# A fixed turn on TensorE for convolution backward and weight-gradient jobs, with reloads moved ahead of transposes and swapped spectra read from memory

## The chip, the cores and the metric

The kernel runs on one core of a Trainium2 chip. The metric is the device time of one execution in microseconds (us); the median of several runs is given, and one further view, the profile, is of a single execution. The engines are named as in the profile: PE (TensorE, matrix multiply), PEld (its weight loads), DVE (VectorE), ACT (ScalarE), POOL (GpSimd) and SP (SyncE, which here only issues DMAs).

## The reference

The program computes the forward pass of four residual layers, and all gradients: for the input, for the two convolution inputs and kernels, and for the two matrices of the dense layer. Sequence length S is 2048, width D is 448, hidden width F is 1792, all in bf16.

```python
def _A_ref(q, k, v, shift_k, ssm_k, ssm_D):
    k_shift = sum of 4 shifted copies of k, each times a column of shift_k
    kv = k_shift * v
    # causal convolution over 2048 steps, by FFT of length 4096
    y = irfft(rfft(kv, 4096) * rfft(ssm_k, 4096))[:2048] + kv * ssm_D
    return q * y
def _B_ref(x, w1, w2):
    return silu(x @ w1) @ w2

x = A_q
x = x + _A_ref(layernorm(x), A_k, A_v, A_shift_k, A_ssm_k, A_ssm_D)
x = x + _B_ref(layernorm(x), B_w1, B_w2)
x = x + _A_ref(layernorm(x), ...same...)
x = x + _B_ref(layernorm(x), B_w1, B_w2)
outputs: x, and the gradients of A_q, A_k, A_v, A_shift_k, A_ssm_k, A_ssm_D, B_w1, B_w2
```

The convolution branch doesn't depend on x, so its result y (in the code `Y`) is computed once and used by both A layers; the gradients of both A layers meet in one array, `gYb`, before a single backward convolution.

## The kernel before, in words

The program has three parts that follow one another in the code.

**Prefix** (`_ssm_prefix`): the forward convolution. A two-stage transform turns the convolution kernel and kv into spectra `spec_K` and `spec_KV`, which are kept in device memory, and `Y` stays in SBUF.

**Main** (`Main.run`): the sequence is cut into 4 chunks of 512 steps (c = 0 to 3), each of 4 tiles of 128 (tl = 0 to 3). A first loop over c does the first A and B layers; it stores the pre-activation of the dense layer as `DT_d` and the activations `aT`, turned by a transposing DMA, as `A_d`. A second loop over c does the second A and B layers forward (`h`, `out`) and at once backward (`ga`, `gn`, with L = 1). A third loop over c does the backward of the first A and B layers (`ga`, `gn`, with L = 0); I call it the **second backward**. In one chunk of it:

- `load_d` reloads a half of `DT_d` into a `dTl` buffer (3 buffers, tag "D"), and `slope` turns it into the derivative of silu: 4 ACT instructions in place. The code calls the first half of chunk c+1 `e0`, the second half `d1`.
- `ga` runs 7 steps fp: PE multiplies (`ps_g`), ACT copies the product out of PSUM (`ghp`, one buffer), DVE multiplies by the derivative (`ghT`). After steps 3 and 6 `store_turned` issues two transposing DMAs on SP's queue and, delayed, the store to `GH_d`.
- `gn` multiplies by the other matrix (`ps_n`), and for each of the 4 tiles runs the backward of both layernorms: ACT `lb_u` and `lb_v`, DVE the rest. The last DVE write of interest is `gYb`.

**Suffix** (`_ssm_suffix`): the backward convolution from `gYb` and the **weight-gradient jobs**. The convolution goes through these steps: stage 1 (`ps_s` with `M1s`, 16 steps n2, one for each 128 rows, n2 = 12 to 15 being chunk 3); 7 groups of transposes (`ps_tr`); then 7 passes cp, each a `spectrum` (`ps_s` with `Gsb`) and an `inverse`, which multiplies the spectrum by the stored ones (DVE `pa`, `pb`) and transforms back (`ps_v`); then `gK`, `gkv`, the shift-kernel gradient `sk`, and a DVE loop for the gradient of k. A job is one row block of a weight gradient: a 512 KB `dstat` tile is loaded from `A_d` or `GH_d` on SP's queue, and 16 matmuls (`ps_d`, 128x448) follow. There are 28 jobs for B_w2 (`_gw2`: moving operands `X` and `GO`) and 28 for B_w1 (`_gw1`: `mov3` and `mov1`), 896 matmuls in all. In the text of the kernel the jobs stand after the convolution.

The order of instructions on each engine is made when the program is built: a scheduler takes instructions by priority as their inputs become free in its own model, and each engine then runs its list strictly in that order. `tc.issue_after(ins)` puts the instructions of a block behind `ins` on that engine's list, without a wait. Before the change no such order links convolution and jobs; the scheduler put job matmuls where it saw room: 55 of the 896 stand ahead of stage 1 of the convolution. DMAs of SP and of ACT go through hardware queues; those of POOL through a software queue.

Of the kernel before, what the change touches and what calls it, by code (L numbers as in the profile page):

```python
# [13 lines left out]
ALU = mybir.AluOpType  # L14
# [19 lines left out]
def make_fft_consts():  # L34
# [44 lines left out]
    GiBc = np.roll(GiBc, 64, axis=0)  # L79
# [127 lines left out]

def _fft_stage1(k, n2, rhs, A1, psum):
    nc = k.nc
    ps = psum.tile([P, 2, 512], FP32, name="ps_s1", **k.pt["s1"])  # L210
    for c in range(2):
        nc.tensor.matmul(ps[:, c, :D], lhsT=k.M1sb[:, n2, c, :], rhs=rhs, start=True, stop=True)
    _copy(nc, k.bal.pick(2 * D), A1[:, :, :, n2, :].rearrange("p dh c ds -> p c dh ds"), ps[:, :, :D].rearrange("p c (dh ds) -> p c dh ds", ds=4))

# [249 lines left out]
class Main:  # L464
# [98 lines left out]
    def h(self, c, L, nT, half, hold):  # L563
# [3 lines left out]
        hold.append((aT, dT))  # L567
        for ft0, n, at in ((0, 2, 1), (2, 2, 0), (4, 2, None), (6, 1, None)) if half == 0 else ((7, 1, None), (8, 2, 1), (10, 2, 0), (12, 2, None)):
# [20 lines left out]
        if L == 1:  # L589
            self.store_turned(k.A_d[1], aT, c, half)  # L590

# [24 lines left out]
    def ga(self, c, L, gT, dT, mid=None):  # L616
        nc, k = self.nc, self.k
        ghT = [self.td.tile([P, NF // 2, 512], BF16, name=f"ghT{h}", tag="T", bufs=3) for h in range(2)]
        for fp in range(NF // 2):
            ps = k.psum.tile([P, 2, 512], FP32, name="ps_g", tag="mm", bufs=2)  # L620
            self.contract(ps, self.w2T, gT, 2 * fp, 2, None if fp == 6 else (fp + 1) % 2)
            if fp == 2 and mid:
                mid()
# [3 lines left out]
            k.bal.add("dve", -0.5)  # L627
            for u in ((0, 1),) if fp != 3 else ((0,), (1,)):
# [3 lines left out]
            if fp in (3, 6):  # L632
                hh = (fp - 3) // 3
                self.store_turned(k.GH_d[L], ghT[hh], c, hh)
        return ghT
# [71 lines left out]
    def run(self):  # L707
# [21 lines left out]
        for c in range(4):  # L729
            gb, gT = self.g_pre(c, 1)  # L730
            self.h(c, 1, nT, 1, cur)
# [3 lines left out]
            self.turn_plain(c)  # L735
            if c == 3:
                d0 = self.load_d(0, 0)
                self.slope(d0)
                k.GO = k.wk.tile([P, NT, D], BF16, name="GO", tag="WA")
                with self.tc.issue_after(k.d_load.ins):  # L740
                    nc.sync.dma_start(out=k.GO[:], in_=_pm(k.grad_out[0]))
            box = []
            ghT = self.ga(c, 1, gT, cur, (lambda: box.append(self.b_pre(c + 1, 3))) if c < 3 else None)
# [5 lines left out]
            else:  # L749
                d1, e0 = self.load_d(0, 1), self.load_d(1, 0)  # L750
# [5 lines left out]
        for c in range(4):  # L756
# [3 lines left out]
            ghT = self.ga(c, 0, gT, dT, (lambda: self.slope(e0)) if c < 3 else None)  # L760
            if c < 3:
                d0, d1 = e0, self.load_d(c + 1, 1)
                if c < 2:
                    e0 = self.load_d(c + 2, 0)
                gn = self.g_pre(c + 1, 0)
            self.gn(c, 0, ghT, nb, lambda tl: self.X[:, 4 * c + tl, :], na)
            if c < 3:
                with self.tc.issue_after(k.d_load.ins):
                    nl = self.load_n(c + 1)
        self.flush()  # L770


def _job(k, ps, src, ft, mov, slot, start, stop):
    pl, tag, bufs = slot
    st = pl.tile([P, NT, P], BF16, name="dstat", tag=tag, bufs=bufs)
    k.nc.sync.dma_start(out=st[:], in_=src[:, ft, :, :])
    for t in range(NT):
        i = k.nc.tensor.matmul(ps[:, :D], lhsT=st[:, t, :], rhs=mov[:, t, :], start=start and t == 0, stop=stop and t == NT - 1)  # L778
    return i


def _gw2(k, pool, fts, slots, bufs=2):
    nc = k.nc
    for ft in fts:
        ps = k.psum.tile([P, 512], FP32, name="ps_d", tag="tr", bufs=2)
        for L, mov in ((0, k.X), (1, k.GO)):
            slot = slots.pop(0)
            slots.append(slot)
            _job(k, ps, k.A_d[L], ft, mov, slot, L == 0, L == 1)
# [5 lines left out]
def _gw1(k, pool, slots, mov3, mov1):  # L795
    nc, psum = k.nc, k.psum
    out7v = k.outs[7].rearrange("(c p) f -> p c f", p=DC)

# [9 lines left out]
    for ft in range(NF):  # L808
        ps = psum.tile([P, 512], FP32, name="ps_d", tag="tr", bufs=2)
        for L, mov in ((1, mov3), (0, mov1)):  # L810
            slot = slots.pop(0)
            slots.append(slot)
            i = _job(k, ps, k.GH_d[L], ft, mov, slot, L == 1, L == 0)
            if hold:
                with k.tc.issue_after(i.ins):
                    turn(*hold)
                hold = None
# [6 lines left out]
def _ssm_suffix(k):  # L824
# [7 lines left out]
    with ExitStack() as es:  # L832
        pool = lambda name: es.enter_context(tc.tile_pool(name=name, bufs=1, reuse_waits="tile"))
        sp0 = pool("sp0")
        k.M1sb = sp0.tile([P, 16, 2, P], BF16, name="M1s", tag="kk0")
        with tc.high_priority():
            nc.gpsimd.dma_start(out=k.M1sb[:].rearrange("p a c k -> p (a c k)"), in_=k.m1_h.ap())
        sp = pool("sspec")
        k.Minvsb = sp.tile([P, 16, 2, P], BF16, name="Minvs")
        dp2 = pool("dp2")  # L840
# [190 lines left out]
```

## Time and profile before

| What | Value |
|---|---|
| Median of 7 runs | 788.89 us (785.77 to 814.69) |
| The profiled execution | 788.5 us, of which its span 786.7 us |
| Busy in the span | PE 719.1 us (91%), DVE 515.3 (65%), ACT 441.3 (56%), POOL 101.7 (13%) |
| Granted TensorE clock, mean | 0.974 |
| DMA | 183.69 MB, mean 233 GB/s |
| Second backward | about 386 to 527 us of the span |
| Stage 1 and transposes of the backward convolution | 532 to 565 us |
| Spectrum and inverse, 7 passes | 565 to 634 us |
| gK, gkv, sk | 634 to 672 us |
| Jobs alone on PE | 672 to 778 us |

Times in the stretches are microseconds from the start of the span. A matmul's record is longer than its share of the engine, because matmuls overlap: a 128x448 matmul is listed with some 352 ns, but the next one starts about 189 ns later. So "PE busy" doesn't say that PE ran at its peak, and start-to-start times are used below wherever a matmul is priced.

### The profile page before, as it was taken

Reading aid. Unit: us, or ns where it says so; the run is one execution under the profiler, and the core shown is the slowest. Engines: PE = TensorE matmul, PEld = TensorE weight load, DVE = VectorE, ACT = ScalarE, POOL = GpSimd, SP = SyncE. Lnnn points to the kernel's source line nnn. Section 1 sums busy time; section 2 is a strip of 40 time slices with the busy share of each in tenths; the row PEclk is TensorE's granted clock in tenths of the full one; section 3 lists DMA queues with packets and bytes.
Section 4 is the critical chain, followed back from the end, with each engine's and each line's share of the span. In section 5 each row is a group of like instructions: output and inputs, shape, how many; then the busy total and the mean of one; then the engine's idle time right before and its main releaser. Section 6 shows DMA issues by size and latency. Waiting matters only on the chain.

```text
span 786.7 us, 12702 instructions
## 1 busy us (share of the span) xinstructions
PE 719.1 (91%) x4982; PEld 380.2 (48%) x5025; DVE 515.3 (65%) x1056; ACT 441.3 (56%) x551; POOL 101.7 (13%) x169
## 2 busy tenths in 40 slices
PE   6998779999999999999987898997979999999995
PEld 4966434444443444434432343443656775545553
DVE  4789678788434977859457877887456635796110
ACT  5889777766566576876846666644536654000000
POOL 1143112222100010000000000010101123111111
PEclk9999889999999999999998999998989999999999
DMA  9369999999977879979997987986978776687650
GB/s 325 131 180 302 378 213 305 296 279 205 245 204 154 174 189 216 228 160 217 339 272 231 237 214 199 296 198 215 404 229 268 253 261 226 180 307 229 185 179 18
DMA packets 188888, 183.69 MB, mean 233 GB/s; under 512 B 135482, under 2 KB 164030, under 8 KB 187804
## 3 DMA queue, kind: packets, MB, share of 16 engines
q1 hardware_dynamic: 173664, 120.93, 59.3%
q0 software_dynamic: 12832, 53.92, 19.3%
q10 hardware_dynamic: 2332, 8.03, 3.3%
q8 instruction: 39, 0.64, 0.3%
q14 instruction: 21, 0.17, 0.1%
HBM read 76.50 MB, written 65.87 MB: 181 GB/s over the span
## 4 chain that ended last, share of the span: by engine, by line
PE 34%; DVE 19%; issue 18%; ACT 14%; DMA 10%; POOL 3%; SPq 0%; POOLq 0%; DVEq 0%; ACTq 0%
PE ps_o L598 6%; PE ps_h L518 6%; PE ps_d L778 6%; PE ps_g L518 3%; PE ps_n L666 3%; DVE dT L113 3%; ACT ghp L625 3%; DMA dTl<-DT_d 2%; DVE lb_junk L641 2%; DMA kk_c<-spec_KV 2%; PE ps_v L232 2%; PE ps_v L233 2%; DVE lb_u L652 2%; DVE ghT L630 2%; ACT na L274 2%
## 5 line engine op out<-in xcount | busy, mean ns | idle before, releaser
L778 PEld LDWEIGHTS <-dstat 128*128 128x128 bf16 x896 | 86.7, 99 | 85.4 <-issue 7.1
L518 PE MATMUL ps_g<-gT,w2T 128*128 128x512 bf16 (+1 forms) x432 | 99.4, 386 | 18.8 <-ACT ghp L625 17.1
L518 PE MATMUL ps_h<-nT,w1sb 128*128 128x512 bf16 (+1 forms) x434 | 102.6, 385 | 6.1 <-DVE dT L113 2.6
L666 PE MATMUL ps_n<-w1T,ghT 128*128 128x448 bf16 x448 | 94.2, 356 | 0.9 <-ACT lb_u L668 0.4
L598 PE MATMUL ps_o<-w2sb,aT 128*128 128x448 bf16 x448 | 90.8, 353 | 1.0 <-ACT aT L574 1.0
L778 PE MATMUL ps_d<-mov,dstat 128*128 128x448 bf16 x448 | 87.2, 352 | 1.0 <-DMA mov<-N_d 1.0
L574 ACT ACTIVATE aT<-ps_h 128x1024 bf16<-128x1024 f32 (+1 forms) x64 | 58.4, 919 | 37.4 <-PE ps_h L518 28.6
L113 DVE CAST dT<-ps_h 128x1024 bf16<-128x1024 f32 (+1 forms) x56 | 59.3, 1064 | 26.5 <-ACT aT L574 26.4
L518 PEld LDWEIGHTS <-w2T 128*128 128x128 bf16 (+1 forms) x448 | 36.3, 97 | 78.2 <-issue 47.4
L625 ACT CAST ghp<-ps_g 128x1024 bf16<-128x1024 f32 x56 | 56.6, 1010 | 30.5 <-DVE ghT L630 18.3
L518 PEld LDWEIGHTS <-w1sb 128*128 128x128 bf16 (+1 forms) x448 | 36.3, 97 | 68.3 <-issue 40.4
L666 PEld LDWEIGHTS <-ghT 128*128 128x128 bf16 x448 | 42.2, 98 | 45.5 <-issue 4.9
L598 PEld LDWEIGHTS <-aT 128*128 128x128 bf16 x448 | 42.1, 98 | 43.7 <-issue 4.3
L778 PE MATMUL ps_d<-X,dstat 128*128 128x448 bf16 x224 | 53.9, 370 | 3.8 <-DMA dstat<-A_d 3.6
L804 ACT COPY do<-ps_dt 112x512 bf16<-112x512 bf16 x14 | 8.2, 587 | 81.8 <-PE ps_dt L802 81.8
L232 PE MATMUL ps_v<-Gsb,pa 128*128 128x128 bf16 x336 | 42.7, 221 | 10.3 <-DVE Zg L113 5.2
L778 PE MATMUL ps_d<-GO,dstat 128*128 128x448 bf16 x224 | 49.6, 353 | 0.2
L233 PE MATMUL ps_v<-Gsb,pb 128*128 128x128 bf16 x336 | 41.7, 221 | 1.0 <-DVE pb L443 0.7
L819 DVE CAST dout<-ps_d 128x448 bf16<-128x448 f32 x14 | 8.7, 622 | 51.5 <-PE ps_d L778 51.5
L232 PEld LDWEIGHTS <-pa 128*128 128x128 bf16 x336 | 33.2, 99 | 12.4 <-DVE pa L442 7.0
L668 ACT ACTIVATE lb_u<-ps_n,rstd 128x448 f32<-128x448 f32 x32 | 20.3, 635 | 33.3 <-DVE X L653 12.0
L630 DVE TENSOR_TENSOR ghT<-dT,ghp 128x1024 bf16<-128x1024 bf16 (+1 forms) x32 | 19.5, 619 | 27.7 <-ACT ghp L625 27.7
(188 smaller groups left out, 1181.2 us busy)
## 6 DMA issues: line engine op xcount, KB each, us to landing
GH_d<-turned SPq DMA_DIRECT2D x16, 896.0 KB, 5.9
dstat<-A_d SPq DMA_DIRECT2D x28, 512.0 KB, 6.5
dstat<-GH_d SPq DMA_DIRECT2D x28, 512.0 KB, 3.7
A_d<-turned SPq DMA_DIRECT2D x12, 896.0 KB, 4.8
DT_d<-dT POOLq DMA_DIRECT2D x8, 896.0 KB, 6.5
dTl<-DT_d SPq DMA_DIRECT2D x8, 896.0 KB, 6.6
spec_K<-Z POOLq DMA_DIRECT2D x7, 512.0 KB, 7.5
KB<-Z POOLq DMA_DIRECT2D x14, 256.0 KB, 11.9
```

Source lines behind the costliest of these rows:

```text
L113: eng.tensor_copy(out, in_)
L232: nc.tensor.matmul(pv[:, i, :], lhsT=pa[:, i * P:(i + 1) * P], rhs=k.Gsb[:, ga, :], start=True, stop=False)
L233: nc.tensor.matmul(pv[:, i, :], lhsT=pb[:, i * P:(i + 1) * P], rhs=k.Gsb[:, gb, :], start=False, stop=True)
L274: nc.scalar.activation(n_g[:, tl, :], src(tl), ACT.Identity, bias=nmr[:, tl:tl + 1], scale=r[:, tl:tl + 1])
L518: self.nc.tensor.matmul(ps[:, u, :], lhsT=w[lo:hi, b, f:f + P], rhs=x[lo:hi, b, :], start=(seen[u] == 1), stop=(seen[u] == ND))
L574: last = nc.scalar.activation(a, ps[:, 0:n, :], ACT.Silu)
L598: nc.tensor.matmul(po[:, :D], lhsT=aT[ft // 7][0][:, ft % 7, tl * P:(tl + 1) * P], rhs=self.w2sb[:, ft, :], start=(ft == 0), stop=(ft == N ...
L625: k.last_gh = nc.scalar.copy(gh[:], ps[:])
L630: nc.vector.tensor_tensor(out=ghT[hh][:, o:o + len(u), :], in0=dT[hh][1][:, o:o + len(u), :], in1=gh[:, u[0]:u[0] + len(u), :], op=ALU.mult)
L666: nc.tensor.matmul(pn[:, :D], lhsT=ghT[ft // 7][:, ft % 7, tl * P:(tl + 1) * P], rhs=self.w1T[:, ft, :], start=(ft == 0), stop=(ft == NF - 1))
L668: last_u = nc.scalar.activation(u0[:], pn[:, :D], ACT.Identity, scale=k.rstd[2 * L + 1][:, t:t + 1], accum_out=cp[:, tl, 0:1])
L778: i = k.nc.tensor.matmul(ps[:, :D], lhsT=st[:, t, :], rhs=mov[:, t, :], start=start and t == 0, stop=stop and t == NT - 1)
```

## The change

It has five edits.

1. **Reloads ahead of transposes.** In `ga` the reload of the derivative half that is needed next is issued after step 3 (and after step 6), before the transposing DMAs of that step; before, it was issued after `ga`. In the second loop's last chunk `d0` is loaded inside `h`. The load of `GO` moves from there into the second backward (chunk 0), and `M1s` is loaded on SP's queue in chunk 2, in the place of `w2sb`, instead of on POOL at the suffix's start.
2. **Held derivative passes.** What `ga` calls in its middle (`slope(e0)`, or the layernorm of the next chunk) now stands behind the `ghp` copy of step 2 on ACT's list, and after it in the program.
3. **The plain transposes** `turn_plain` are issued two each in chunks 0 and 1 instead of one in each chunk.
4. **A fixed turn.** Every PE block of the suffix is chained to the one before (`_in_turn`), and job matmuls are drawn from a generator in fixed numbers between convolution blocks (`weave(n)`): 4 to 10 after each step of stage 1, 3 after each group of transposes, 2 after each half of a spectrum, 5 after each of the 28 inverse blocks, and so on. One row block (32 matmuls) stays free ahead of it.
5. **Swapped stored spectra.** The product with swapped halves used a swapped copy of the new spectrum, made by two DMAs from SBUF to SBUF for each pass (`xsw_c`). Now the stored spectra are read twice, once plainly and once with halves swapped, and the constant `GiBc` is no longer rolled. The loads of `Minvs`, `ksf`, `gks` and `mov3` are queued behind these reads. Stage 1's copies of the first 12 steps go to ACT.

```diff
@@ class Main
-    def ga(self, c, L, gT, dT, mid=None):
+    def ga(self, c, L, gT, dT, mid=None, loads=(None, None)):
...
-            if fp == 2 and mid:
-                mid()
             gh = self.ch.tile([P, 2, 512], BF16, name="ghp", tag="ghp", bufs=1)
             k.last_gh = nc.scalar.copy(gh[:], ps[:])
...
+            if fp == 2 and mid:
+                with self.tc.issue_after(k.last_gh.ins):
+                    mid()
...
             if fp in (3, 6):
                 hh = (fp - 3) // 3
+                if loads[hh]:
+                    ld.append(self.load_d(*loads[hh]))
                 self.store_turned(k.GH_d[L], ghT[hh], c, hh)
...
-            self.h(c, 1, nT, 1, cur)
+            d0 = self.h(c, 1, nT, 1, cur, (lambda: self.load_d(0, 0)) if c == 3 else None)
...
-            self.turn_plain(c)
+            if c < 2:
+                self.turn_plain(2 * c)
+                self.turn_plain(2 * c + 1)
...
-            ghT = self.ga(c, 0, gT, dT, (lambda: self.slope(e0)) if c < 3 else None)
+            ghT = self.ga(c, 0, gT, dT, (lambda: self.slope(e0)) if c < 3 else None, ((c + 1, 1) if c < 3 else None, (c + 2, 0) if c < 2 else None))
...
+                    if c == 0:
+                        nc.sync.dma_start(out=k.GO[:], in_=_pm(k.grad_out[0]))
+                    if c == 2:
+                        k.M1sb = k.wk.tile([P, 16, 2, P], BF16, name="M1s", tag="WB")
+                        nc.sync.dma_start(out=k.M1sb[:].rearrange("p a c k -> p (a c k)"), in_=k.m1_h.ap())
@@ the fixed turn
+@contextmanager
+def _in_turn(k):
+    bb = k.nc.cur_bb.bb
+    with ExitStack() as es:
+        if k.tail is not None:
+            es.enter_context(k.tc.issue_after(k.tail))
+        n = len(bb.instructions)
+        yield
+    pe = k.pe_engine
+    for i in reversed(bb.instructions[n:]):
+        if i.engine == pe:
+            k.tail = i
+            break
@@ def _ssm_suffix
+        def weave(n):
+            with _in_turn(k):
+                for _ in zip(range(n), jobs):
+                    pass
...
         for n2 in range(16):
-            _fft_stage1(k, n2, k.gYb[:, n2, :], A1, psum)
+            with _in_turn(k):
+                _fft_stage1(k, n2, k.gYb[:, n2, :], A1, psum, nc.scalar if n2 < 12 else None)
+            weave(4 if n2 < 8 else 8 if n2 < 11 else 10)
...
             def spectrum(cp):
-                kk = (sp0.tile([P, 2, 2048], ...) if cp % 2 else p1.tile([P, 2, 2048], ...))
-                xsw = p1.tile([P, 2048], BF16, name="xsw_c", tag="xsw", bufs=2)
-                nc.gpsimd.dma_start(out=t[0], in_=k.SPEC_d["K"][:, lo:hi])
-                nc.gpsimd.dma_start(out=t[1], in_=k.SPEC_d["KV"][:, lo:hi])
+                t = p1.tile([P, 4, 2048], BF16, name="kk_c", tag="kk", bufs=2)
+                for i, nm in enumerate(("K", "KV")):
+                    nc.gpsimd.dma_start(out=t[:, i, :], in_=k.SPEC_d[nm][:, lo:hi])
+                    kv = _swap_halves_dma(k, t[:, 2 + i, :], k.SPEC_d[nm], lo, hi, nc.gpsimd, dlo=0)
+                with tc.issue_after(kv.ins):
+                    if cp == 1:
+                        _load_minv(k, nc.gpsimd)
+                    if cp == 2:
+                        nc.gpsimd.dma_start(out=ksf[:], in_=_pm(k.KS_d[:]))
+                    if cp == 3:
+                        nc.gpsimd.dma_start(out=gks[:], in_=v_pm)
+                    if cp == NCI // 2 - 1:
+                        nc.gpsimd.dma_start(out=k.mov3[:], in_=_pm(k.N_d[3][:]))
...
-                _swap_halves_dma(k, t[2], Zf, lo, hi, nc.scalar, dlo=0)
...
-                        nc.vector.tensor_tensor(out=pb[:], in0=t[2][:, o], in1=spec_t[:, o], op=ALU.mult)
-                        _fft_inv_stage2_chunk(k, pa, pb, True, B1, ci, psum, cnd=cnd)
+                        nc.vector.tensor_tensor(out=pb[:], in0=Zf[:, ci * 1024:(ci + 1) * 1024], in1=t[:, 2 + i, o], op=ALU.mult)
+                        with _in_turn(k):
+                            _fft_inv_stage2_chunk(k, pa, pb, True, B1, ci, psum, cnd=cnd)
+                        weave(5)
```

## The prediction

> **What bounds the kernel now.** I read the page's first part, then PE's waits, then stretches, then ACT and SP in order of time around the longest waits.
>
> ```profile
> PE 719.1 (91%) x4982; PEld 380.2 (48%) x5025; DVE 515.3 (65%) x1056; ACT 441.3 (56%) x551; POOL 101.7 (13%) x169
> ```
>
> PE is the busiest engine. The work after the change is the same on PE, matmul for matmul, so the time can only move by what PE waits or by its clock. PE's waits (us in total, times, longest), from 386 to 532 us for the first line and over the whole span for the others:
>
> ```profile
> PE ps_g L518 <- ACT ghp L625: 15.2, 8, 8.1
> ...
> PE ps_v L232 <- DVE Zg L113: 5.2, 1, 5.2
> ...
> PE ps_d L778 <- DMA dstat<-A_d: 3.6, 1, 3.6
> ```
>
> The stretches show what follows a wait (length, busy time of PE, PEld, DVE, ACT and POOL, clock, DMA share, GB/s):
>
> ```profile
> 414.00:422.00 8.00, 3.43 (x13) 1.06 (x13) 5.26 (x13) 6.58 (x10) 0.00 (x0) 0.57 0.83 307
> 479.00:484.00 5.00, 5.00 (x18) 2.10 (x17) 4.68 (x16) 5.00 (x9) 0.00 (x0) 0.66 0.86 206
> 536.00:546.00 10.00, 6.46 (x21) 2.78 (x22) 4.51 (x10) 3.27 (x5) 0.55 (x1) 0.66 0.56 194
> 556.00:575.00 19.00, 13.54 (x144) 9.31 (x143) 8.51 (x9) 7.24 (x6) 1.61 (x4) 0.92 1.01 393
> 571.00:579.00 8.00, 4.00 (x13) 1.78 (x14) 4.10 (x6) 0.00 (x0) 0.00 (x0) 0.57 0.80 237
> 575.00:634.00 59.00, 58.57 (x602) 41.08 (x607) 36.69 (x59) 35.47 (x40) 7.73 (x15) 0.97 0.71 225
> 671.00:778.00 107.00, 106.00 (x596) 56.21 (x594) 51.59 (x72) 9.61 (x17) 16.98 (x27) 1.00 0.64 200
> ```
>
> Each long wait is followed by half clock: 0.43 of 8 us is 3.4 us lost, 0.34 of 5 is 1.7, 0.34 of 10 is 3.4, 0.43 of 8 is 3.4. From 671 us on PE is full with jobs alone, so every microsecond saved earlier arrives at the end. ACT and SP in order of time name the causes:
>
> ```profile
> 398.52 1.27 SPq L690 DMA_DIRECT2D dTl<-DT_d  x1
> ...
> 402.23 6.40 SPq L484 DMA_TRANSPOSE turned<-ghT  x2
> 408.72 0.88 SPq L690 DMA_DIRECT2D dTl<-DT_d  x1
> ```
>
> ```profile
> 415.00 1.06 ACT L560 ACTIVATE dTl<-dTl 128x1024 bf16<-128x1024 bf16 x1 [7.52 <-DMA dTl<-DT_d]
> ...
> 417.52 1.00 ACT L625 CAST ghp<-ps_g 128x1024 bf16<-128x1024 f32 x1
> ```
>
> The reload of e0 stands behind two transposes; its slope stands ahead of the `ghp` copies on ACT; so PE waits 8.1 us for a copy whose own inputs were there. In the suffix the first stored spectra are late (the chain):
>
> ```profile
> 556.01 16.42 DMA kk_c<-spec_KV
> ```
>
> **What the Trainium skill says.** "TensorE: Matmul & The Clock Gate", Part 1: about 3.4 us without work drops PE to half rate. The trace agrees after the waits of 8.1, 3.6 and 5.2 us; the loss at 479 us follows no such wait. The same page's Part 1 on queue depths: ACT runs strictly in order, which the 7.52 us above show. "DMA: Bandwidth & Descriptors", Bandwidth: about 358 GB/s between device memory and a core. The trace has 393 GB/s with all engines busy (556 to 575 us), so I use 393.
>
> **The change part by part.** Unit prices, start to start, from PE in order of time: 128x448 matmul 0.19 us (16 in 3.0), 128x128 0.056, 128x512 0.21.
>
> *Second backward (edits 1 and 2).* One reload earlier by the transposes in front of it: in the built order d1 passes one transpose, e0 one more per half; at 402.23 two took 6.4 us of SP, so e0 of the first chunk comes some 7 us earlier, at about 408. Its slope now stands behind three `ghp` copies, so these no longer wait. Of the 15.2 us I let 12 go and keep 3, since slopes still occupy ACT (four instructions, 3.5 us) between copies. The reload's own wait on SP is for the `ghT` product that frees its buffer; the transpose and the `GH_d` store behind it need that product anyway. The half clock there goes: 3.4 + 1.7 = 5.1. Only 32 job matmuls instead of 55 now stand ahead of stage 1: 23 x 0.19 = 4.3 us of filler are done later. Net 12.2 + 5.1 - 4.3 = **13.0**. Can the other engines follow? `lb_u` of a chunk's first tile starts at 399.7, 434.2, 464.3, 494.2 and 520.7 us: 30 us for a chunk. A chunk needs PE 7 x 1.5 + 56 x 0.19 + 16 x 0.056 = 22 us, DVE 23 (stretches of 30 us), ACT 17 to 22. So 26 us is possible, and what is late next is DVE's layernorm chain at 4.7 us a tile.
>
> *Suffix.* (a) The `dstat` wait of 3.6 with its half clock 3.4: two transposes and a queue of loads stood before that load; M1s, 1 MB, leaves their company for chunk 2. (b) The wait for the spectra, 5.2, with 3.4: the first reads no longer stand behind M1s, Minvs and ksf on POOL, nor beside gks; in the built order they wait for the last `GH_d` store and the last `lb_v`, some 20 us ahead of need. (c) The wait of `ps_r`, 1.0, gets 10 jobs in front. Sum **16.6**. The 14 swap DMAs leave ACT's queue; ACT isn't on the path there, so this is worth nothing.
>
> *What it adds.* (d) d0's slope in the second loop's last chunk stands in the built order before the second tile's `lb_u` (357.6 us), while its load is issued only behind chunk 2's last transposes (end on SP 353.7) and needs 6.6 us to land: ACT stands until about 361, and behind it `lb_u`, `gT` and the `aT` that PE's `ps_h` needs. PE loses about 3.5, and 1.5 come back where ACT is then ahead at the first `ps_g`: **+2** (0 to 5). (e) Stage 1's first 12 copies are on ACT alone, between `lb_u` and `lb_v`, which wait for DVE: a step has 6 matmuls, 1.1 us on PE, and a copy 0.9 on ACT, but ACT stands 1.5 to 1.7 at each of some three such places (as at 530.9 and 533.2 now), and the third row block's `dstat` is behind the last transposes: **+3** (0 to 6). (f) Each pass now reads 2.1 MB on POOL in 6 DMAs (before 1.05 MB, and 0.5 within SBUF), while PE needs 4 x 0.21 + 4 x 0.19 for the spectrum and 4 x (16 x 0.056 + 5 x 0.19) for the inverse: 9.0 us a pass. With two buffers the reads of five passes start only when the pass two before is multiplied. In these five passes move 5 x 2.1 + ksf and gks 3.7 + 7.5 `dstat` of 0.52 and stores, 4.8: 19 MB. At 393 GB/s 48 us, against 45 on PE: **+4**. Bounds: 0, since DVE may run three blocks ahead; 15 at the 317 GB/s that 225 at a share of 0.71 gives. The queue order adds to it: the K spectrum is read first, KV is used first. Minvs, ksf, gks and mov3 behind them aren't needed before `gK`. (g) The turn itself: before, PE took jobs while a block was late in the model; now only the fixed number. ACT (6 copies of 1.02 and 0.5: 6.6) and DVE (8 products of 0.69: 5.5) are below 9.0, so small bubbles: **+2** (0 to 4). (h) Two plain transposes each in chunks 0 and 1 (2.6 us of SP each) delay the release of turned tiles there and free chunks 2 and 3: nothing (0 to 1), since SP is idle for some 9 us in such a chunk (328.9 to 337.5). GO's and M1s's loads land tens of us before use: nothing.
>
> Sum against the profiled execution: 788.5 - 13.0 - 16.6 + 2 + 3 + 4 + 2 = **769.9**. It stands 0.4 below the median of the runs, so the median is forecast at 770.
>
> **The rivals.** *Clean (0.12):* reads and copies hide; d to g cost 3: 762 to 758. For it: PE passes 575 to 634 now with 58.57 of 59 us busy. Against: 393 GB/s were reached for 19 us only. *Reads bind (0.17):* the convolution becomes a DMA stage at 317 GB/s: +11 more, and half clock after one or two of the waits, 3: 784. For it: twice the bytes in the shortest stage. *The held passes move nothing (0.05):* e0's load is slow because of DMA traffic (share 0.98 or more around 410 us), not because of SP's order, and the scheduler's list makes ACT wait elsewhere: the 13.0 go down to 3 or 4: 779. *Slower (0.08):* the fixed turn at the inverse blocks. Where spectra are late, the jobs behind them on PE's list are held too. A pass has some 12.4 us between release and use (one block 1.85, one pass 9.0, a spectrum 1.6); the first two passes' reads now, also 2 MB, took 16.4 us beside gks and ksf. At that duration each of five passes waits 4 us and brings a half-clock window of up to 3.4: 20 to 37 us instead of 4. The sum turns positive from about 17 us a read on (earlier if every wait halves the clock): some 795. Against it: the 16.4 us had 3.7 MB more beside them. The likeliest case keeps 0.58, 763 to 778.
>
> **How the numbers follow.** A measurement of this kernel can tell about 0.3% (2.4 us) from no change. Cases below 786.5: likeliest, clean, held passes, and nine tenths of reads-bind: 0.87 in all. Same 0.04, slower 0.09. The range 755 to 788 leaves out the slower case and the tails.
>
> **What would show it.** Right: PE waits for `ghp` in the second backward sum to less than 5 us and its chunks come 26 to 27 us apart; no wait of `ps_v` for `Zg` near 5; the clock is 1.00 where the named waits were. Ahead of `sk` stand 62 more job matmuls than before (419 for 357 in the built orders), so `sk` ends at 668 + 12 - 19 = 661 us, and the last stretch of jobs alone is 12 us shorter; the DVE loop of 48 us (672 to 720) still lies beside it. Wrong: `pa` or `pb` on DVE waits for `kk_c` over 10 us in sum, with PE standing in `ps_v`; ACT stands over 5 us before d0's slope; `ps_s` waits for `A1g`. The forecast fails if the inverse passes come 12 us apart or more.

## The result, and the profile after

The kernel after takes **798.18 us** (median of 25 runs, 793.79 to 800.68); the kernel before, run beside it on the same chip, 790.55 us. The ratio is **1.0088, with a 95% interval of 1.0072 to 1.0105**: slower by 0.9%, where 770 us had been forecast. Medians are of all executions, while ratios leave out the slow ones, which lie over 1.5% above the fastest of the same kernel. The profiled execution of after has a span of 795.5 us (before 786.7).

First part of the page, after:

```profile
PE 718.9 (90%) x4981; PEld 383.0 (48%) x5025; DVE 509.8 (64%) x1051; ACT 446.7 (56%) x556; POOL 116.9 (15%) x197
```

PE does the same work as before, so again only its waits and its clock count. Its waits after (us in total, times, longest): the first line from 386 to 532 us, the others from 540 to 800 us.

```profile
PE ps_g L517 <- ACT ghp L625: 5.3, 12, 1.4
...
PE ps_v L231 <- DVE pa L936: 10.5, 3, 7.1
PE ps_v L232 <- DVE pb L937: 7.0, 3, 2.9
PE ps_dt L834 <- DVE dout L851: 4.1, 5, 2.3
PE ps_gK L976 <- DVE gK L112: 2.5, 1, 2.5
PE ps_sk L1025 <- issue: 2.3, 1, 2.3
PE ps_d L807 <- DMA dstat<-A_d: 0.6, 1, 0.6
```

The 15.2 us of `ghp` have become 5.3, the longest wait 1.4 in place of 8.1; the `dstat` wait is 0.6 in place of 3.6. What is new stands in the inverse (`ps_v` behind `pa` and `pb`) and behind it. Stretches after (length, busy time of PE, PEld, DVE, ACT, POOL, clock, DMA share, GB/s):

```profile
416.00:424.00 8.00, 7.65 (x47) 3.53 (x47) 6.72 (x16) 6.88 (x8) 0.00 (x0) 1.00 0.75 198
540.00:559.00 19.00, 17.60 (x169) 11.59 (x169) 9.78 (x10) 8.44 (x8) 4.89 (x9) 1.00 1.04 274
559.00:644.00 85.00, 67.21 (x625) 46.85 (x630) 36.72 (x59) 38.59 (x42) 20.69 (x39) 0.86 0.93 270
585.00:595.00 10.00, 1.44 (x7) 0.48 (x5) 2.13 (x4) 1.93 (x2) 2.71 (x6) 0.67 1.04 292
605.00:615.00 10.00, 5.13 (x30) 3.08 (x29) 5.08 (x8) 2.89 (x4) 4.20 (x8) 0.69 1.03 277
691.00:785.00 94.00, 89.82 (x503) 46.66 (x501) 51.47 (x73) 8.16 (x14) 15.46 (x24) 1.00 0.60 192
```

The place of the old 8 us hole (416 to 424) is full and at full clock. The inverse, 59 us long before, is 85 long: in it PE is busy for 67 us at a clock of 0.86. The DMA engines are full there, but at 270 GB/s, where the kernel before had moved 393 at a share of 1.01 (556 to 575 us). DVE in order of time, with the idle time ahead of each group in brackets, says what is awaited:

```profile
592.49 1.90 DVE L936 TENSOR_TENSOR pa<-Zg,kk_c 128x1024 bf16<-128x1024 bf16 x3 [12.89 <-DMA kk_c<-spec_KV]
...
608.11 1.89 DVE L936 TENSOR_TENSOR pa<-Zg,kk_c 128x1024 bf16<-128x1024 bf16 x3 [9.59 <-DMA kk_c<-spec_KV]
```

These and two smaller ones (4.83 and 3.92) are 31.2 us; `pb` waits another 4.4. From the first issue of a pass's reads to its first product lie 21.1, 21.6, 13.2 and 15.4 us in these four passes. POOL's queue shows reads that are also issued late:

```profile
581.39 0.56 POOL L916 DMA_DIRECT2D gks<-in_A_v_dram  x1 [6.54 <-DMA ksf<-KS_d]
...
586.51 0.53 POOL L908 DMA_DIRECT2D kk_c<-spec_K  x1 [3.94 <-DMA kk_c<-spec_K]
...
605.32 0.59 POOL L822 DMA_DIRECT2D out_dram<-dout  x1 [9.85 <-ACT dout L821]
605.90 0.54 POOL L908 DMA_DIRECT2D kk_c<-spec_K  x1
```

In these lines issues wait for the landing of earlier DMAs, and the sixth pass's reads stand behind a store that waits for its job.

For a balance I count what PE loses: for each matmul the time to the next one's start, less its price at full clock (close to the unit prices of the prediction), where it is longer. The places are us from the start of each kernel's span; "reads left out" is an experiment below.

| PE's loss, us | before | after | reads left out |
|---|---|---|---|
| to 370 us | 69.3 | 71.1 | 71.1 |
| 370 to 530 (second backward) | 35.4 | 23.7 | 23.7 |
| 530 to 650 | 22.1 | 31.1 | 11.6 |
| 650 to 710 | 6.4 | 12.3 | 12.7 |
| from 710 | 1.9 | 3.9 | 2.8 |
| sum | 135.1 | 142.1 | 121.9 |

The second backward gained 11.7 us. From 530 to 650 us, where the old waits of the suffix are gone, the loss is still 9.0 larger, and behind it 7.9 larger.

### The profile page after: what moved, and what is told of

The parts are those of the page before. It is cut to its first block, busy times and chain, and to the rows that moved or that the text cites. A ratio compares the mean times of both kernels' runs of the same rounds, so it can differ in the third digit from the quotient of the medians.

```text
span 795.5 us, 12689 instructions
## 1 busy us (share of the span) xinstructions
PE 718.9 (90%) x4981; PEld 383.0 (48%) x5025; DVE 509.8 (64%) x1051; ACT 446.7 (56%) x556; POOL 116.9 (15%) x197
## 4 chain that ended last, share of the span: by engine, by line
PE 27%; DVE 27%; DMA 15%; issue 15%; ACT 12%; POOL 3%; SPq 1%; POOLq 0%; DVEq 0%; ACTq 0%
PE ps_o L599 6%; PE ps_h L517 6%; PE ps_d L807 5%; DVE lb_junk L646 4%; DVE dT L112 3%; DVE ghT L633 3%; DVE lb_u L657 3%; ACT ghp L625 3%; DMA gks<-in_A_v_dram 2%; DVE lb_u L686 2%; PE ps_n L671 2%; DMA kk_c<-spec_KV 2%; DMA ksf<-KS_d 2%; ACT na L273 2%; DMA KB<-Z 1%
## 5 line engine op out<-in xcount | busy, mean ns | idle before, releaser
L517 PE MATMUL ps_g<-gT,w2T 128*128 128x512 bf16 (+1 forms) x431 | 97.4, 380 | 9.1 <-ACT ghp L625 7.2
L671 PE MATMUL ps_n<-w1T,ghT 128*128 128x448 bf16 x448 | 92.6, 353 | 1.0 <-DVE ghT L633 0.4
L517 PEld LDWEIGHTS <-w1sb 128*128 128x128 bf16 (+1 forms) x448 | 36.5, 97 | 67.9 <-issue 40.0
L231 PE MATMUL ps_v<-Gsb,pa 128*128 128x128 bf16 x336 | 47.6, 231 | 15.7 <-DVE pa L936 10.5
L807 PE MATMUL ps_d<-GO,dstat 128*128 128x448 bf16 x224 | 53.0, 362 | 0.8 <-DMA dstat<-A_d 0.6
L232 PE MATMUL ps_v<-Gsb,pb 128*128 128x128 bf16 x336 | 46.5, 232 | 8.0 <-DVE pb L937 7.0
L231 PEld LDWEIGHTS <-pa 128*128 128x128 bf16 x336 | 35.0, 104 | 21.7 <-DVE pa L936 11.8
L936 DVE TENSOR_TENSOR pa<-Zg,kk_c 128x1024 bf16<-128x1024 bf16 x28 | 18.6, 687 | 37.5 <-DMA kk_c<-spec_KV 31.2
L232 PEld LDWEIGHTS <-pb 128*128 128x128 bf16 x336 | 34.7, 104 | 15.4 <-DVE pb L937 7.8
## 6 DMA issues: line engine op xcount, KB each, us to landing
KB<-Z POOLq DMA_DIRECT2D x14, 256.0 KB, 11.7
```

Of the source, the lines that this page charges most:

```text
L231: nc.tensor.matmul(pv[:, i, :], lhsT=pa[:, i * P:(i + 1) * P], rhs=k.Gsb[:, ga, :], start=True, stop=False)
L232: nc.tensor.matmul(pv[:, i, :], lhsT=pb[:, i * P:(i + 1) * P], rhs=k.Gsb[:, gb, :], start=False, stop=True)
L517: self.nc.tensor.matmul(ps[:, u, :], lhsT=w[lo:hi, b, f:f + P], rhs=x[lo:hi, b, :], start=(seen[u] == 1), stop=(seen[u] == ND))
L671: nc.tensor.matmul(pn[:, :D], lhsT=ghT[ft // 7][:, ft % 7, tl * P:(tl + 1) * P], rhs=self.w1T[:, ft, :], start=(ft == 0), stop=(ft == NF - 1))
```

## The experiments

Three theories stood at the start. **T1**: the doubled reads are late and hold PE. **T2**: the fixed turn holds PE. **T3**: the last stretch of jobs (93.2 us, before 88.6) is longer because the loop for the gradient of k has come to lie beside the `dout` copies on DVE. Every time below is a median, and the ratio is to the kernel before on the same chip; for after it is 1.0088. That kernel's median was between 790.6 and 794.3 us beside the various runs, so two times can differ by some 4 us from the chip alone; where that matters, the ratios are compared.

### The swap made in SBUF again

```diff
-                t = p1.tile([P, 4, 2048], ...)
+                t = p1.tile([P, 3, 2048], ...)
                 for i, nm in enumerate(("K", "KV")):
-                    nc.gpsimd.dma_start(out=t[:, i, :], in_=k.SPEC_d[nm][:, lo:hi])
-                    kv = _swap_halves_dma(k, t[:, 2 + i, :], k.SPEC_d[nm], lo, hi, nc.gpsimd, dlo=0)
+                    kv = nc.gpsimd.dma_start(out=t[:, i, :], in_=k.SPEC_d[nm][:, lo:hi])
...
+                _swap_halves_dma(k, t[:, 2, :], Zf, lo, hi, nc.scalar, dlo=0)
...
-                        (pb: in0=Zf[...], in1=t[:, 2 + i, o])
+                        (pb: in0=t[:, 2, o], in1=t[:, i, o])
```

> The kernel after, with edit 5's data part undone: each pass reads K and KV once (2 DMAs of 0.5 MB), and the swapped copy is again made of the new spectrum inside SBUF by two DMAs on ACT's queue. The fixed turn, the second backward and the places of Minvs, ksf, gks and mov3 stay. Theory T1 (the doubled reads on POOL's queue are late, and hold PE): the inverse, 84 us from the first to the last ps_v in the kernel after, falls to about 62 (7 passes of 9.0 us), DVE's waits of 31 us for kk_c nearly go, and the time falls by some 20 us to 775 to 780. Theory T2 (the fixed turn itself costs the time: jobs held behind late blocks, copies too late for the fixed number of jobs): the inverse stays above 75 us, PE then waits for the swaps or for copies, and the time stays above 790. Theory T3 (the jobs of B_w1, 93 us against 89 before, because DVE's loop for the gradient of k now lies beside them) holds with either and is worth 4 us at most.

Measured: 791.53 us, ratio 0.9992 (0.9962 to 1.0021). The inverse takes 75 us from its first `ps_v` to its last (some 73 from the first `pb` on, the number that a later expectation uses). T2's numbers came, if barely, and not T1's: the waits for reads are gone as T1 said, but others have come in their place. DVE's longest wait from 540 to 650 us:

```profile
DVE pb L938 <- DMA kk_c<-Zg: 24.7, 6, 7.7
```

The swap of the new spectrum, one pass ahead, is itself too late. This doesn't show that the turn is the cause: without the turn, in a version below, the inverse is as long.

### Edits 1 to 3 alone

```diff
 (the kernel before, with after's ga, h and loops; of the suffix only:)
-        k.M1sb = sp0.tile([P, 16, 2, P], BF16, name="M1s", tag="kk0")
-            nc.gpsimd.dma_start(out=k.M1sb[:].rearrange(...), in_=k.m1_h.ap())
```

> The kernel before with edits 1 to 3 alone (reloads ahead of transposes, held derivative passes, plain transposes, M1s and GO loaded earlier on SP's queue); the suffix is the old one, without a fixed turn, and its first spectra no longer stand behind M1s on POOL's queue. T1: the second backward ends some 11 us earlier and all of it arrives: 776 to 780. T2: as T1 here, since there is no turn. A third theory (what the second backward gains is only borrowed from the filler jobs, and comes back at the end): no less than 787.

Measured: 796.21 us, ratio 1.0022 (0.9995 to 1.0049): nothing arrives. The third theory gave the number, but not for its reason. The chain shows it:

```profile
546.73 27.75 DMA kk_c<-spec_KV
```

The second KV spectrum is read behind `ksf` and `mov3` and beside `gks`; it lands at 574.5, and the first `ps_v` comes at 575 as in the kernel before. What was gained ahead is spent on a wait of 16.1 us there.

### The turn taken out of after

```diff
 def _in_turn(k):
-    (chain to k.tail)
+    yield
...
         def weave(n):
+            if n < 100:
+                return
```

> The kernel after, with edit 4 undone: no block is chained to another, and all jobs but the first row block stand behind the convolution in the text, for the scheduler to place. The doubled reads stay. T1: the reads bind the inverse as before; the scheduler can put other jobs in while a block is late in its model only, so the time stays within 5 us of the 798 of after, and DVE's waits for kk_c stay near 30 us. T2: the time falls by over 10 us, to 788 or less, although DVE still waits for kk_c.

Measured: 812.01 us, ratio 1.0235 (1.0188 to 1.0282). Neither range came: the kernel is some 12 us slower than after by the ratios (14 by the times). T2 falls as the cause, since with the same late reads and no turn it gets worse. DVE's `pa` waits for `kk_c` as long (31.2 us); between 530 and 650 us PE loses 47 us instead of 31, and its B_w1 jobs begin at 703 instead of 691.

### The swapped reads left out

```diff
                 for i, nm in enumerate(("K", "KV")):
-                    nc.gpsimd.dma_start(out=t[:, i, :], in_=k.SPEC_d[nm][:, lo:hi])
-                    kv = _swap_halves_dma(k, t[:, 2 + i, :], k.SPEC_d[nm], lo, hi, nc.gpsimd, dlo=0)
+                    kv = nc.gpsimd.dma_start(out=t[:, i, :], in_=k.SPEC_d[nm][:, lo:hi])
...
-                        (pb: in1=t[:, 2 + i, o])
+                        (pb: in1=t[:, i, o])
```

> The kernel after with the four swapped reads of each pass left out; the second product of a pair uses the plain spectrum once more, so the transforms back are not those of the reference. The fixed turn and all instructions on PE, DVE and ACT are those of after; there are no swap DMAs of any kind. It prices the extra reads alone. T1: the inverse falls to 60 to 63 us and the time to 772 to 778, and it lies within 3 us of the version with swaps inside SBUF. T2: 790 or more. If only ksf and gks among the reads were the cause, the time falls by less than half of that, since they stay where they are.

Measured: 775.14 us, ratio 0.9784 (0.9752 to 0.9816); the inverse 59 us, no wait for `kk_c`. So the swapped reads cost **23 us** (798.2 less 775.1; 24 by the ratios), T1 holds, and the fixed turn runs an inverse without such waits when nothing is late. The version with swaps in SBUF, expected within 3 us of this one, is 16 above it, by its late swaps.

### Six small reads, half the bytes

```diff
                 for i, nm in enumerate(("K", "KV")):
-                    (one read of 128 rows, then the swapped reads)
+                    for a, b in ((0, 64), (64, 96), (96, 128)):
+                        kv = nc.gpsimd.dma_start(out=t[a:b, i, :], in_=k.SPEC_d[nm][a:b, lo:hi])
```

> Leaving out the swapped reads took the kernel after from 798 to 775. This one also leaves them out (the second product uses the plain spectrum again), but reads the two plain spectra in three pieces each: six DMAs a pass on POOL's queue as in the kernel after, at half its bytes. If the bytes are the cost (the transfers of a 60 us stretch don't fit beside each other), it stays at 773 to 779. If the number of DMAs is the cost (POOL's issues stand behind one another and behind the finished transfer whose semaphore they take), it goes to 785 or more, and POOL shows waits of several us between the issues of one pass.

Measured: 779.54 us, ratio 0.9830 (0.9760 to 0.9899). The number of DMAs alone isn't the 23 us. But DVE waits for KV again, 15.0 us in sum, at half the bytes; so pieces, which here span 64 and 32 partitions, aren't free.

### Minvs, gks and ksf behind the last reads

> The kernel after with Minvs, gks and ksf, 4.7 MB, moved from between the reads of passes 1 to 3 to behind the reads of the last pass, ahead of mov3; the doubled reads stay. If the sum of bytes in the stretch is the limit, the first passes gain what the late loads no longer take, 4.7 MB at some 300 GB/s, 15 us less about 5 for what gK and gkv then wait for: 785 to 792. If the reads' own length (buffers come free one pass ahead, then six transfers) is the limit, less than 4 us change: 794 to 800, and DVE's waits for kk_c stay above 25 us.

Measured: 797.14 us, ratio 1.0064 (1.0032 to 1.0096). The sum changed by less than 4 us, but not as the second case had it. In the profile the inverse takes 71 us instead of 84, and DVE's waits for KV fall from 35.6 us to 24.7 (16.8 and 7.9 of `pa` and `pb`): the first passes did gain what the late loads no longer take. The gain is lost behind the inverse. There the load `sk_all`, 4.6 us of waiting in after, keeps DVE for 19.0 us beside the late loads; ACT's `gK` copy waits for DVE, and PE 11.3 us for that copy. So the other loads of the stretch have a part in what the doubled reads cost, and this run doesn't rule out the sum of bytes.

### Swaps in SBUF, two passes ahead

```diff
-            prev = spectrum(0)
+            kks, xsws = [reads(0)], [spectrum(0), spectrum(1)]
             for cp in range(NCI // 2):
-                cur = spectrum(cp + 1) if cp + 1 < NCI // 2 else None
-                inverse(cp, prev)
-                prev = cur
+                if cp + 1 < NCI // 2:
+                    kks.append(reads(cp + 1))
+                if cp + 2 < NCI // 2:
+                    xsws.append(spectrum(cp + 2))
+                inverse(cp, kks.pop(0), xsws.pop(0))
```

> The swaps inside SBUF again, with the fixed turn (that version took 791.5 beside 793.5 of the kernel before), but each spectrum and its swap are made two passes ahead of their use instead of one, with three xsw buffers; the reads stay one pass ahead. If its 12 us over the version without swaps (inverse 73 us against 61) come from the swap's way (copies out of PSUM, issue on ACT, 5.3 us in flight) being longer than one turn of a pass, DVE's waits for the swap, 24.7 us, fall below 6, the inverse to 62 to 64 and the time to 777 to 781. If the fixed turn or the traffic is the cause, it stays above 787.

Measured: 784.37 us, ratio 0.9891 (0.9850 to 0.9933). Between the cases: the waits for the swap are gone from the head of DVE's list, and one of 10.2 us for KV has come (5.4 us on PE). The inverse took 68 us.

### Swaps in SBUF, one pass ahead, no turn

> The swaps inside SBUF one pass ahead, without the fixed turn: edits 1 to 3 and only the earlier place of the reads from edit 5 remain, the scheduler places the jobs. If the fixed turn is what makes the late swap visible (in the kernel before the inverse took 58 us with the same swaps), the inverse takes 58 to 62 us, the first ps_v comes near 560, and the time is 774 to 780. If the reads, not the turn, set it: 788 or more. The version with edits 1 to 3 alone, whose first spectra landed 27.8 us after issue behind ksf, mov3 and gks, took 796.

Measured: 785.21 us, ratio 0.9929 (0.9897 to 0.9962), 5 to 6 us below the version with the turn and between the two cases. The first `ps_v` comes at 550, but the inverse takes 74 us, as long as with the turn, since DVE waits 31.9 us for the swaps. So what the missing turn gains isn't gained in the inverse; a table below counts where.

### The same bytes in whole transfers

```diff
-                    kv = _swap_halves_dma(k, t[:, 2 + i, :], k.SPEC_d[nm], lo, hi, nc.gpsimd, dlo=0)
+                    kv = nc.gpsimd.dma_start(out=t[:, 2 + i, :], in_=k.SPEC_d[nm][:, lo:hi])
```

> The kernel after, with its bytes but not its pieces: each stored spectrum is read twice by whole transfers over 128 partitions (4 DMAs of 0.5 MB a pass instead of 2 of 0.5 and 4 of 0.25). The second copy isn't swapped, so the transforms back are not those of the reference. In the kernel after the software queue moved 18.2 MB between 555 and 635 us in 81% of 16 engines' time, 281 GB/s; with half the bytes in whole transfers 12.35 MB in 40%, 389 GB/s. If the bytes alone are the cost, it stays at 794 to 800. If the pieces are slow (the version with half the bytes in six pieces moved 303 GB/s), the queue goes at 350 GB/s or more and the time falls to 780 to 788.

Measured: 781.0 us, ratio 0.9825 (0.9783 to 0.9868). This is the run that divides the 23 us: the bytes are 6 of them (781.0 less 775.1), the form of the transfers is the other 17. By the ratios it is 3 and 21, and the intervals of this run and of the one without swapped reads overlap, so the bytes' part is small and not exact.

### The dout copies of the B_w1 jobs on ACT

```diff
-        nc.vector.tensor_copy(o[:], ps[:, :D])
+        nc.scalar.copy(o[:], ps[:, :D])
```

> The kernel after, with the copies of the B_w1 jobs out of PSUM (dout, 14 of them) on ACT instead of DVE, where the loop for the gradient of k lies at the same time. If that loop is what makes the last stretch of jobs longer (93.2 us against 88.6 in the kernel before, PE waits 4.1 us in ps_dt for dout), PE's waits there go and the time falls by 3 to 5 us, to 793 to 795. If not: within 1 us of 798.

Measured: 794.94 us, ratio 1.0011 (0.9987 to 1.0035). T3 holds: the stretch is 88.2 us, the waits of `ps_dt` fall to 0.7. The medians differ by 3 us, the ratios by 0.0077, which is 6.

### Two ahead, with both small edits, with and without the turn

> Spectra and swaps two passes ahead with the fixed turn (784.4), and two things more: the dout copies of the B_w1 jobs on ACT, and KV read before K, since KV is used first. If the parts are independent, 4 us less for the first and up to 5 for the second (PE waited 6.2 us for products that waited for KV): 776 to 780. If KV's read was late because of the traffic and not of the order, 779 to 782.

> As the last, with KV first, but without the fixed turn: blocks and jobs are placed by the scheduler (then the loop for the gradient of k lies ahead of the B_w1 jobs, so dout stays on DVE). With swaps one pass ahead the fixed turn cost 6 us (791.5 with it, 785.2 without). If that cost came only from swaps that were late, this version equals the one with the turn, 776 to 781. If the turn costs in itself, it is 4 us or more below it; if the turn is worth something once nothing is late, 4 or more above.

Measured: with the turn 778.83 us, ratio 0.9802 (0.9771 to 0.9833); without it **775.41 us, ratio 0.9753 (0.9719 to 0.9787)**. Both beat both kernels; the second is 2.5% below before. It is edits 1 to 3, the spectra's reads ahead of the other loads with KV first, and swaps two passes ahead. It also keeps stage 1's first copies on ACT. Two lines of its PE waits from 500 to 800 us are its longest:

```profile
PE ps_v L232 <- DVE pa L934: 4.4, 3, 2.5
PE ps_dt L825 <- DVE dout L842: 2.3, 3, 1.4
```

The second case is the nearer one: the turn costs 3.4 us by the medians. The intervals of the two ratios overlap a little, but on one chip five of the second's six executions (773.8 to 776.2 us) lie below all six of the first's (777.5 to 780.0). The versions differ in the engine of the `dout` copies too.

Three pairs of versions now differ in the turn. PE's loss, counted as above but by each kernel's own stages, with the turn and without it (behind the inverse is from the last `ps_v` to the end):

| PE's loss, us | stage 1 and transposes | inverse | behind the inverse |
|---|---|---|---|
| doubled reads (798, 812) | 4.0, 4.1 | 28.0, 36.5 | 15.8, 13.8 |
| swaps one pass ahead (792, 785) | 7.9, 2.6 | 15.5, 20.9 | 19.4, 11.2 |
| swaps two passes ahead (779, 775) | 6.3, 2.9 | 8.6, 14.0 | 14.7, 9.7 |

In each pair the turn saves 5 to 9 us in the inverse. With the swaps it loses 8 to 14 us ahead of it and behind it. A version with the turn in the inverse alone wasn't run.

### Swapped reads in whole transfers

```diff
-    k.SPEC_d = {nm: dram.tile([128, SPEC], ...
+    k.SPEC_d = {nm: dram.tile([192, SPEC], ...
...
+                nc.gpsimd.dma_start(out=k.SPEC_d["K"][128:192, lo:hi], in_=Ka[0:64, lo:hi])
...
-                    kv = _swap_halves_dma(k, t[:, 2 + i, :], k.SPEC_d[nm], lo, hi, nc.gpsimd, dlo=0)
+                    kv = nc.gpsimd.dma_start(out=t[:, 2 + i, :], in_=k.SPEC_d[nm][64:192, lo:hi])
```

> A full kernel with the doubled reads in whole transfers: the spectra are stored with rows 0 to 63 once more below row 127 (14 stores of 0.25 MB more in the prefix), so the swapped read is rows 64 to 191 in one transfer over 128 partitions. If the halves are what is slow: 780 to 786 (781 for whole transfers, and 0 to 5 us for the stores in the prefix, where the first slices show a DMA share of 0.9 in one slice alone). If reading rows into other partitions is slow: above 792.

> As the last, with KV's two reads ahead of K's, and the dout copies of the B_w1 jobs on ACT (794.9 against 798.2 for that alone). Parts independent: 3 us less for the copies, 0 to 2 for the order: 3 to 5 us below the last.

Measured: 805.44 us (six executions from 791 to 816, so no ratio is given) and 804.28 us, ratio 1.0127 (1.0073 to 1.0182). Both times miss, but not in the inverse. Two stretches within the second one's inverse:

```profile
595.00:605.00 10.00, 9.95 (x100) 6.90 (x100) 7.35 (x11) 6.45 (x7) 3.15 (x6) 1.00 1.02 419
605.00:615.00 10.00, 9.95 (x109) 7.17 (x107) 5.46 (x9) 6.49 (x9) 2.79 (x6) 1.00 1.02 417
```

At 419 and 417 GB/s its whole inverse takes 60 us, with the halves swapped (62 in the first). The time goes earlier: its first `ps_v` comes at 585, 26 us later than in after. With the added stores on POOL's queue the main part begins 5 us later. Then PE waits 20.0 us in one piece, behind an `aT` that waits 25.1 us for a transposing DMA. By SP's queue its transposes stand behind the spectra's stores: SP waits 22.3 us for `spec_KV` (7.9 in after) and starts the first of them 15 us later. Two of them then take long, `w1T` 18.6 us (6.6 in after) and the first `turned` 15.9 (3.5). Why they do wasn't settled.

### The dout stores on ACT's queue

```diff
-        nc.gpsimd.dma_start(out=k.outs[8][ft * P:(ft + 1) * P, :], in_=o[:])
+        nc.scalar.dma_start(out=k.outs[8][ft * P:(ft + 1) * P, :], in_=o[:])
```

> The kernel after with the 14 stores of the B_w2 jobs (dout) issued on ACT's queue, just behind the copy that they store, instead of POOL's, where the reads of the sixth pass stood 9.85 us behind one that waited for its job. If such holds are a part of the 23 us, the time falls by 4 to 8 us, to 790 to 794. If the reads are bound by their transfers, they only wait elsewhere: 796 to 800.

Measured: 799.97 us, ratio 1.0103 (1.0054 to 1.0152): the reads that stood behind stores only wait elsewhere. POOL's waits for `dout`, 48.2 us in after, are gone, but those for the buffers that `pb` frees rise from 10.2 us to 33.6.

### Halves, but not swapped

```diff
+def _halves_dma(k, dst, src, lo, hi, eng):
+    eng.dma_start(out=dst[0:64, :], in_=src[0:64, lo:hi])
+    return eng.dma_start(out=dst[64:128, :], in_=src[64:128, lo:hi])
...
-                    kv = _swap_halves_dma(k, t[:, 2 + i, :], k.SPEC_d[nm], lo, hi, nc.gpsimd, dlo=0)
+                    kv = _halves_dma(k, t[:, 2 + i, :], k.SPEC_d[nm], lo, hi, nc.gpsimd)
```

> The kernel after with its bytes, its number of DMAs and its transfers over 64 partitions, but rows 0 to 63 go to partitions 0 to 63 and rows 64 to 127 to 64 to 127: nothing is swapped. So the second copy is a plain one and the transforms back are not those of the reference. If transfers over 64 partitions are what is slow: 794 to 800 as the kernel after, the software queue near 280 GB/s of its own time between 555 and 635 us, DVE's waits for kk_c near 31 us. If the crossing is: 779 to 785, as the version with whole transfers (781).

Measured: 801.17 us, ratio 1.0113 (1.0066 to 1.0159). So it is the transfer over 64 partitions that is slow, not the crossing. The software queue between 555 and 635 us (packets, MB, share of 16 engines' time), in this run, in after, with whole transfers, and with the swapped reads left out:

```profile
q0 software_dynamic: 4000, 17.12, 80.9%
```

```profile
q0 software_dynamic: 4054, 18.21, 80.9%
```

```profile
q0 software_dynamic: 3750, 17.40, 53.9%
```

```profile
q0 software_dynamic: 2411, 12.35, 39.7%
```

The bytes of the first three are nearly the same. Bytes over share and 80 us give the rate while the queue's packets run: 17.12 / (0.809 x 80 us) = 265 GB/s, then 281, then 404. In packets: 0.809 x 16 x 80 us / 4054 = 255 ns each in after, 184 ns with whole transfers, at like sizes (4.5 and 4.6 KB). Less the last line, the transfers over 64 partitions alone come to an estimated 145 GB/s in this run and 178 in after, the added whole ones to some 445.

One rival is argued away, not tested: the version with whole transfers issues four DMAs a pass, this one and after six. The DMA engines are busy through the whole 80 us in after (share 1.01), so they didn't lack work for want of issues; but six whole transfers of the same bytes weren't run.

## Why the prediction was wrong

**The step that failed is (f).** It counted the bytes rightly and priced them at 393 GB/s, a rate that the kernel before reaches almost only with whole transfers. Half of the bytes that a pass now reads come in transfers over 64 partitions, and POOL's queue with this mixture runs at 281. +4 (0 to 15) became 23: 17 or more for the form, 6 or less for the bytes, so for the bytes alone the step was near. The prediction's own signs of being wrong came with it: 31 us of `pa` waiting for `kk_c`, and inverse passes 12 us apart (84 us for seven). The Trainium skill has what was missing: "SBUF — State Buffer", section "Door 1: The DMA port swizzle", gives 196 GB/s for partitions 0 to 63 against 328 for all 128, measured at 1 MiB, because 64 partitions in one block reach half of the ports. The section "Can I just issue two DMAs to hit both halves?" adds that "The only way to hit all 16 ports is one transfer spanning all 128 partitions." The runs agree that such transfers are slow: 255 ns for a packet against 184, 798 us against 781. The ports themselves no run here shows. With the page's price the step's own sum would have been 13.75 MB at 393 plus 5.25 MB at 196: 35 + 27 = 62 us against 45 on PE, an estimate of +17. A sign stood on the page of the kernel before, in the prefix, where the swaps `KB` are pairs of transfers over 64 partitions within SBUF. They took longer than stores of twice the bytes (KB each, median us from issue to landing, waiting in the queue included):

```profile
spec_K<-Z POOLq DMA_DIRECT2D x7, 512.0 KB, 7.5
KB<-Z POOLq DMA_DIRECT2D x14, 256.0 KB, 11.9
```

**The slower rival** gave 795 and came within 3 us. Its mark, some 17 us from release to use, was passed in two passes (21.1 and 21.6 us), and half clock followed as it said. Its other half is wrong: the turn isn't what makes late reads costly, since without it the kernel is 12 to 14 us slower. The "reads bind" rival (784) had the right engine, the DMA, and a rate, 317 GB/s, that was still too high.

**The second backward** was forecast at 13.0. PE's loss there fell by 11.7, the `ghp` waits to 5.3 (forecast 3, and under 5 as a mark), and the half clock is gone: right in mechanism and nearly in size. The chunks came 28 us apart (30 before, 26 to 27 forecast). That it could arrive nowhere was not foreseen: with the old suffix it doesn't, because the spectra then land late.

**The suffix.** (a) and (b) were right: the `dstat` wait is 0.6, the wait of 5.2 for `Zg` before the first `ps_v` is gone. (c) was right for `ps_r`, but the reuse of a `gK` buffer took its place with 2.5. The sum of the gains counts some time twice. It charges the half clock for the whole of each stretch, 3.4 us for 8 us at 0.57, though PE was busy for only 3.43 of these 8 us and the rest is the wait that is already counted. Half clock costs at most half of the busy time, so 1.7, 3.2 and 2.0 us for the three stretches that follow a wait: 6.9 in place of 10.2.

**The added terms.** (d) +2: 1.8 more loss up to 370 us, and ACT waited 1.5 us for d0's load, not over 5. But versions that are alike up to there differ by 7 us in that loss, so the 1.8 isn't told from chance. (e) +3: `ps_s` waits 0.8 for `A1g`; too high by about 2. (h) nothing: no run shows a loss. (g) +2 was mis-sized and misplaced. Within the inverse the turn gave no bubble once the reads were out (59 us), but behind it PE's loss grew by 7.9, in waits that the step didn't name: 2.5 at `gK`, 2.3 at `sk`, and the gk loop (the loop for the gradient of k). The text said that this loop "still lies beside" the jobs from 672 to 720; with 16 and 32 job matmuls put ahead of its inputs it starts at 693 and collides with the `dout` copies. That is the 3 to 6 us which the ACT copies gave back.

Without (f), 770 less 4 is 766; the run without the swapped reads took 775 us, or 772 by its ratio, so the other steps were 6 to 9 us too good. (g) is some 6 of these and the time counted twice at least 3; (e), too high, works against them. A slip without effect: the chances named for a time below 786.5 add up to 0.90, not 0.87.

## What to carry to other kernels

A transfer is priced by its bytes and by the partitions that it spans: blocks of 64 partitions cost here far more than their share of the bytes, and a DMA share near 1.0 beside a low GB/s is the sign to look for. An earlier stage's gain arrives only if the next stage's loads are there sooner too; of edits 1 to 3 nothing arrived until the spectra's reads went ahead of the other loads. A fixed interleaving can save in one stage and lose in the next, as in the three pairs above, so count it by stage; here more came from giving the late swaps another pass of lead. And a half clock is charged only over the time in which the engine works.

## What was not expected of the hardware

With half of the reads in transfers over 64 partitions the software queue's packets ran at 265 to 281 GB/s, at DMA shares up to 1.04; with whole ones alone they ran at 404, and the DMA engines together at up to 419 with the halves swapped. Swaps within SBUF, which are also over 64 partitions, land in 5.3 us for 0.25 MB where a whole read of 0.5 MB takes 6.4 (medians of the version with swaps one pass ahead). And 14 stores of 0.25 MB added in the prefix set a kernel back by 26 us before its inverse began: 5 in the prefix and 20 in one wait behind transposing DMAs, two of which took 34 us together instead of 10, for a reason that stays open.
